# The spectrum step of an FFT and soft-MoE kernel, with constant and data exchanged on TensorE

## The chip, the cores and the metric

The kernel runs on one core of a Trainium2 chip. The metric is device time in microseconds (us) of one execution. The engines are called as in the profile: PE is TensorE's matmuls, PEld its weight loads, DVE is VectorE, ACT is ScalarE, POOL is GpSimd, SP is SyncE, whose queue issues the DMA transfers here. A matmul holds one operand still in the array (the weight, up to 128 rows by 128 columns) and streams the other through it; its result lands in PSUM, out of which DVE and ACT read. A float32 matmul shows as two records in the profile.

## The reference

The input x has 8 batches of 2496 rows of 256 numbers. A filter is applied by a Fourier transform over the rows, and a soft mixture of experts is computed from the result y:

```python
X = np.fft.rfft(x, axis=1)
Y = X * (filt_r + 1j * filt_i)[None]
y = np.fft.irfft(Y, n=2496, axis=1).reshape(8 * 2496, 256)

logits = y @ phi                                  # 32 slots: 8 experts x 4
d = exp(logits - logits.max(0)); d /= d.sum(0) + 1e-09
slot_input = (d.T @ y).reshape(8, 4, 256)
slot_out[e] = relu(slot_input[e] @ w1[e]) @ w2[e]   # for every expert e
c = exp(logits - logits.max(1)); c /= c.sum(1) + 1e-09
out = c @ slot_out
```

All of it is float32.

## The kernel before

**The transform.** 2496 is 39 x 64, so a transform over the rows is one of length 39 and one of length 64. The first stage (`first_stage` for batch 0, `s1_unit` at line 356 for the others) does the 39; its result for a batch is 20 values of t by 64 rows by 256 columns, real and imaginary part. For batches 1 to 7 it goes to DRAM and comes back as tiles `ash` with the 64 rows times two parts on 128 partitions; for batch 0 `turn` makes `ash` by transposes.

**The x step.** `x_unit(b, c)` does the second stage for two values of t, ten units per batch and 80 in all. In the kernel before, `ash` is the weight (128 by 128, one half of the columns d at a time) and the constant matrix (`a1` or `b0`, 128 by 128) streams through. The result in PSUM has d on the partitions, and real and imaginary parts of 64 frequencies for each t along the row. Four matmuls of 128 streamed columns make a unit. DVE then multiplies with the filter: two products of 512 columns (lines 455 and 457) and two of 256 columns that add and subtract (458 and 459; in batches 6 and 7 POOL does these two). The result is `yt`, the filtered spectrum with d on the partitions.

**Transposes and logits.** `t_unit(b, c)` transposes `yt` by four matmuls against the identity (line 467), and ACT copies the result to `y` (line 475), the filtered spectrum with frequencies on the partitions. Every second time it also computes the logits of two units: eight matmuls with 32 columns of `phi` as weight and `yt` streaming (line 485), copied by ACT to `lt` (line 495).

**The chain.** `chain(g)` runs for each of five groups of batches, cut into pieces by `yield`: it transposes the logits (ltr), transforms them back to rows (v1, v, lg), takes the maximum and the exponential (mt, mb, d), transforms the result into the frequency domain again (u, u2, dd), and adds up `slot_input` there, as products of `dd` with `y` (s). It never forms y over the rows. In its code all matmuls and transposes go through two helpers, so they have lines 515 and 512 in the profile.

**The order.** The program is written as a loop over slots n, 80 and two more. A slot issues `x_unit(n)`, the first-stage units that `at_slot` gives it, `t_unit(n-2)` with its logits, and one to three chain pieces (`hop_slot`). A scheduler orders the instructions of each engine by a simulated timeline and by priorities; `high_priority` marks the first stage and the logits; `not_before(a, b)` fixes that a comes after b on its engine, and `behind` makes a queue of such instructions. `held` stores the last instruction of a step for such orders. PSUM has two buffers each for x, for t and l together, and for the chain; the first stage has one of two banks. `ypool` holds 34 units of `y` in rotation.

**Signs.** Frequencies above the half need the filter's imaginary part with the other sign. `make_signs` spreads the signs over all partitions by ten matmuls during batch 0's first stage (line 755), ACT copies them (757), and `sign_tables` multiplies the table `ff_t` with them (line 765), the first two units on DVE, the other eight on POOL. The constants come from `shape_constants`, the filter tables from `filter_layout`.

**Start and end.** `keep_warm(WM)` issues two matmuls on zeros before the first data is there (line 313). After the last slot the rest of the chain goes in the order that `TAIL` writes out; then come the experts' matmuls and the output.

Of the kernel before, what the change touches and what calls it, by code (L numbers as in the profile page):

```python
# [56 lines left out]
LT = 2  # L57
# [31 lines left out]
def shape_constants():  # L89
# [51 lines left out]
    put("sgn", sgn.reshape(NT // 2, P))  # L141
# [39 lines left out]
def filter_layout(filt):  # L181

    idx = np.array([[freq_of(t, c) for c in range(N2)] for t in range(NT)])
    a = filt[np.minimum(idx, SEQ - idx)]
    a = np.ascontiguousarray(a.reshape(NT, N2, 2, P).transpose(3, 0, 2, 1))
    return a.reshape(P, NT // 2, 256)
# [66 lines left out]
def fft_soft_moe(ctx, tc, x0, w0, x, ff, phi, wx, cst, w1q, out):  # L253
# [26 lines left out]
    sgn_t = cst_t[:, OFF["sgn"][0] : OFF["sgn"][0] + P]  # L280
# [41 lines left out]
    held = [None, None, None, None, None]  # L322
# [104 lines left out]
    def x_unit(b, c):  # L427
# [3 lines left out]
        ps = ps_x.tile([P, 4, 2, 64], F32, tag="x", name=f"x_{b}_{c}")  # L431
        for k in range(2):
            for dh in range(2):
                ins = pe.matmul(  # L434
                    ps[:, 2 * k + dh].rearrange("q r c -> q (r c)"),
                    ash[:, k, dh * P : (dh + 1) * P],
                    C("a1" if t0 + k else "b0"),
# [10 lines left out]
        frv, fiv = (  # L448
            ff_t[:, c, k].rearrange("q (p o c) -> q p o c", o=1, c=64).broadcast_to([P, 4, 2, 64]) for k in range(2)
        )  # L450
        t2 = prod.tile([P, 4, 2, 64], F32, tag="t2", name=f"t2_{b}_{c}")
        if c % 2 == 0:
            yts[b, c // 2] = prod.tile([P, 2, 4, 2, 64], F32, tag="yt", name=f"yt_{b}_{c}")
        yt = yts[b, c // 2][:, c % 2]
        dve.tensor_tensor(out=t2, in0=ps[:, :, ::-1, :], in1=fiv, op=ALU.mult)  # L455
        add, part = (pool_e, yt) if b >= PA else (dve, ps)
        dve.tensor_tensor(out=part, in0=ps, in1=frv, op=ALU.mult)  # L457
        add.tensor_tensor(out=yt[:, :, 1, :], in0=part[:, :, 1, :], in1=t2[:, :, 1, :], op=ALU.add)  # L458
        add.tensor_tensor(out=yt[:, :, 0, :], in0=part[:, :, 0, :], in1=t2[:, :, 0, :], op=ALU.subtract)  # L459

    def t_unit(b, c):

        yt = yts[b, c // 2]
        pt = ps_t.tile([P, 2, 2, P], F32, tag="t", name=f"t_{b}_{c}")
        for k in range(2):
            for dh in range(2):
                pe.transpose(pt[:, k, dh, :], yt[:, c % 2, 2 * k + dh].rearrange("q r c -> q (r c)"), ident)  # L467
# [7 lines left out]
        act.copy(y, pt.rearrange("k p h d -> k p (h d)"))  # L475
        ys[b, c] = y
        if c % 2 == 1:
            i = c // 2
            if i == 0:
                lts[b] = work.tile([P, 5, P], F32, tag="lt", name=f"lt_{b}", bufs=2)  # L480
            pl = ps_t.tile([P, P], F32, tag="t", name=f"l_{b}_{i}")
            with tc.high_priority():
                for dh in range(2):
                    for j in range(4):
                        ins = pe.matmul(  # L485
                            pl[32 * j : 32 * j + 32, :],
                            phi_t[:, dh, :],
                            yt[:, j // 2, 2 * (j % 2) + dh].rearrange("q r c -> q (r c)"),
                            start=(dh == 0),
                            stop=(dh == 1),  # L490
                        )
                        if j + dh == 0:
                            not_before(ins, held[1])
            held[2] = ins
            act.copy(lts[b][:, i, :], pl)  # L495
# [21 lines left out]
    def chain(g):  # L517
# [134 lines left out]
        TG = SA if nb == 2 else HT // 2  # L652
# [10 lines left out]
        for t0 in range(0, HT, TG):  # L663
            n = min(TG, HT - t0)
            pd = psum([P, TG, 2, nb, SLOTS], f"dd_{g}_{t0}")
# [3 lines left out]
            ended[0] = act.copy(dd[:, t0 : t0 + n], pd[:, 0:n])  # L669
            if t0 != 0:  # L670
                yield "dd"
# [21 lines left out]
        terms = [(ti, th, b2) for ti in range(HT) for th in range(2) for b2 in range(nb)]  # L693
        step = 4 * nb
        for k, (ti, th, b2) in enumerate(terms):
            j = k % 4
            t = th * HT + ti
            pe_m(
                pss[32 * j : 32 * j + 32, :],
                dd[:, ti, th, b2, :],  # L700
                ys[bs[b2], t // 2][:, t % 2, :],
# [46 lines left out]
    signs = []  # L748

    def make_signs(c0):  # L750
        n = min(4, NT // 2 - c0)
        ps = ps_c.tile([P, 4, 2, 1, N2], F32, tag="c", name=f"sgn_{c0}")
        for c in range(n):
            one = ident[:, c0 + c : c0 + c + 1].broadcast_to([P, P])
# [382 lines left out]
```

## Time and profile before

| | |
|---|---|
| Median of 3 runs | 379.02 us (378.91 to 382.27) |
| The profiled execution's own time | 379.5 us |
| Its span, first to last instruction | 377.7 us |
| Mean granted TensorE clock | 0.958 |
| Busy share of PE, PEld, DVE, ACT, POOL | 93, 69, 68, 46, 39% |
| HBM traffic | 63.11 MB read, 40.12 MB written |

By time, the span has four parts: batch 0's first stage and its start up to 19 us, the 80 slots from there to about 282 us, the rest of the chain up to 304 us, and the experts and the output up to 377.7 us.

How the profile is read: a row of a group names the line, the engine, the operation, the tiles (out<-in), for a matmul the rows by columns of its weight and then the streamed shape, the count, busy time and the mean ns of one. Records of matmuls overlap, since they are pipelined; so the mean of one record is longer than the time between two. The chain of waits is the work that ended last, followed back from the end; a piece of it has a start, a duration, and what it is. "Granted clock" is the share of full speed that TensorE was given.

### The profile page before, as it was taken

How to read it: one execution, taken by the hardware profiler on the slowest of the kernel's cores; microseconds unless marked ns; L12 is line 12 of the kernel's file. 1: busy time of each engine (PE TensorE's matmuls, PEld its weight loads, DVE VectorE, ACT ScalarE, POOL GpSimd, SP SyncE). 2: the span in 40 equal slices, each digit the busy share in tenths (PEclk: the TensorE clock that was granted, in tenths of full speed). 3: DMA queues.
4: the chain of work that ended last, by engine and by line, in shares of the span. 5: the costliest groups of instructions: out<-in, count | busy, mean ns of one | idle time of the engine just before them, and what ended most of it. 6: DMA issues, size and time to landing. Idle time of an engine off the chain costs nothing.

```text
span 377.7 us, 10582 instructions
## 1 busy us (share of the span) xinstructions
PE 350.9 (93%) x4274; PEld 260.7 (69%) x4274; DVE 256.6 (68%) x519; ACT 175.4 (46%) x357; POOL 148.9 (39%) x180
## 2 busy tenths in 40 slices
PE   8999899699999989999999999899998999989960
PEld 6977577467677657777776787777876635878850
DVE  1576788495987987589697837766674562787540
ACT  3556545345456443545644454433363430766430
POOL 0098745453461634454253654323521302650000
PEclk9999999999999999999999999899999999999555
DMA  8999799799889685968955848333698994599996
GB/s 303 400 393 278 245 329 361 257 349 339 259 277 325 187 290 177 320 208 271 336 160 151 253 140 297 129 105 92 203 389 247 339 316 104 222 416 415 418 416 288
DMA packets 50151, 103.92 MB, mean 275 GB/s; under 512 B 5218, under 2 KB 23394, under 8 KB 47926
## 3 DMA queue, kind: packets, MB, share of 16 engines
q1 hardware_dynamic: 49412, 102.83, 78.9%
q8 instruction: 34, 0.56, 0.6%
q10 hardware_dynamic: 690, 0.42, 0.4%
q14 instruction: 15, 0.12, 0.1%
HBM read 63.11 MB, written 40.12 MB: 273 GB/s over the span
## 4 chain that ended last, share of the span: by engine, by line
PE 82%; DMA 7%; DVE 4%; ACT 2%; issue 1%; POOL 0%; DVEq 0%; ACTq 0%; SPq 0%
PE x L434 20%; PE t L467 10%; PE s L356 10%; PE l L485 6%; DMA out<-ob 5%; PE s L515 5%; PE u L515 4%; PE v L515 4%; PE s L407 3%; PE lg L515 3%; PE dd L515 2%; PE out L1087 2%; PE h L1031 2%; PE o L1049 2%; DVE ob L1092 2%; PE v L512 2%
## 5 line engine op out<-in xcount | busy, mean ns | idle before, releaser
L434 PE MATMUL x<-cst_t,ash 128*128 128x128 f32 x640 | 87.8, 280 | 6.2 <-DMA ash<-a_dram 4.1
L434 PEld LDWEIGHTS x<-cst_t,ash 128*128 128x128 f32 x640 | 78.1, 191 | 15.0 <-issue 8.3
L455 DVE TENSOR_TENSOR t<-x,ff_t 128x512 f32<-128x512 f32 x80 | 54.8, 687 | 48.6 <-PE x L434 34.2
L335 POOL TENSOR_TENSOR eo<-xt 128x512 f32<-128x512 f32 (+1 forms) x40 | 48.1, 1203 | 93.0 <-issue 89.6
L365 ACT COPY at<-s 128x1024 f32<-128x1024 f32 (+1 forms) x42 | 39.6, 942 | 48.3 <-PE s L356 34.6
L467 PE MATMUL t<-cst_t,yt 128*128 128x128 f32 x320 | 50.8, 281 | 1.5 <-POOL yt L459 1.4
L467 PEld LDWEIGHTS t<-cst_t,yt 128*128 128x128 f32 x320 | 36.2, 141 | 22.6 <-issue 9.8
L338 POOL TENSOR_TENSOR eo<-xt 128x512 f32<-128x512 f32 (+1 forms) x40 | 48.4, 1211 | 0.0
L475 ACT COPY y<-t 128x512 f32<-128x512 f32 x58 | 33.4, 589 | 24.1 <-PE t L467 22.2
L356 PE MATMUL s<-eo,w1q_t 64*64 64x512 f32 (+1 forms) x336 | 42.8, 579 | 0.0
L457 DVE TENSOR_TENSOR x<-x,ff_t 128x512 f32<-128x512 f32 x60 | 41.5, 695 | 1.2
L1087 PE MATMUL out<-so,st 32*128 32x256 f32 x468 | 35.5, 337 | 2.0 <-ACT ob L1092 1.0
L1087 PEld LDWEIGHTS out<-so,st 32*128 32x128 f32 x468 | 31.0, 222 | 5.8 <-ACT ob L1092 2.9
L1092 DVE COPY ob<-out 128x512 f32<-128x512 f32 (+1 forms) x40 | 25.0, 670 | 8.5 <-DMA out<-ob 5.8
L458 POOL TENSOR_TENSOR yt<-yt,t 128x256 f32<-128x256 f32 x20 | 15.0, 752 | 37.0 <-DVE yt L457 25.3
L1092 ACT COPY ob<-out 128x512 f32<-128x512 f32 (+1 forms) x40 | 21.7, 582 | 14.8 <-DMA out<-ob 7.9
L458 DVE TENSOR_TENSOR yt<-x,t 128x256 f32<-128x256 f32 x60 | 25.2, 420 | 1.9 <-PE l L485 0.2
L485 PE MATMUL l<-yt,phi_t 128*32 128x128 f32 x640 | 26.2, 278 | 0.0
L459 DVE TENSOR_TENSOR yt<-x,t 128x256 f32<-128x256 f32 x60 | 24.9, 414 | 0.0
L495 ACT COPY lt<-l 128x128 f32<-128x128 f32 x40 | 10.7, 268 | 30.4 <-PE l L485 30.0
L485 PEld LDWEIGHTS l<-yt,phi_t 128*32 128x32 f32 x640 | 15.4, 109 | 8.6 <-issue 5.3
L515 PE MATMUL s<-y,dd 128*32 128x256 f32 x232 | 19.3, 381 | 0.4 <-ACT dd L669 0.3
(120 smaller groups left out, 492.1 us busy)
## 6 DMA issues: line engine op xcount, KB each, us to landing
xt<-in_x SPq DMA_DIRECT2D x35, 512.0 KB
ash<-a_dram SPq DMA_DIRECT2D x70, 256.0 KB
out<-ob SPq DMA_DIRECT2D x17, 1024.0 KB
a_dram<-at SPq DMA_DIRECT2D x56, 240.0 KB
w<-in_wx SPq DMA_DIRECT2D x33, 256.0 KB
w<-in_wx SPq DMA_DIRECT2D x6, 512.0 KB
x_t<-in_x SPq DMA_DIRECT2D x5, 512.0 KB
ff_t<-in_ff SPq DMA_DIRECT2D x10, 256.0 KB
```

Of the source, the lines that this page charges most:

```text
L335: ins = eng.tensor_tensor(out=eo[:, 0, 0:n], in0=xs[:, :, 0], in1=xs[:, :, 1], op=ALU.add)
L338: ins = eng.tensor_tensor(out=eo[:, 1, 0:n], in0=xs[:, :, 0], in1=xs[:, :, 1], op=ALU.subtract)
L356: ins = pe.matmul(ps, w1q_t[q, c], eo[q, c, 0:n], start=True, stop=True)
L434: ins = pe.matmul(ps[:, 2 * k + dh].rearrange("q r c -> q (r c)"), ash[:, k, dh * P : (dh + 1) * P], C("a1" if t0 + k else "b0"), start=Tr ...
L455: dve.tensor_tensor(out=t2, in0=ps[:, :, ::-1, :], in1=fiv, op=ALU.mult)
L457: dve.tensor_tensor(out=part, in0=ps, in1=frv, op=ALU.mult)
L458: add.tensor_tensor(out=yt[:, :, 1, :], in0=part[:, :, 1, :], in1=t2[:, :, 1, :], op=ALU.add)
L467: pe.transpose(pt[:, k, dh, :], yt[:, c % 2, 2 * k + dh].rearrange("q r c -> q (r c)"), ident)
L485: ins = pe.matmul(pl[32 * j : 32 * j + 32, :], phi_t[:, dh, :], yt[:, j // 2, 2 * (j % 2) + dh].rearrange("q r c -> q (r c)"), start=(dh = ...
L515: line(pe.matmul(*a, **k))
L1087: nc.tensor.matmul(prs[k][:, mm, :], sts[n][q, hs, c0 : c0 + P], so[q, ho], start=(i == 0), stop=(i == 2))
L1092: copy(ob[:, nm * k : nm * (k + 1), :], prs[k])
```

## The change

The x step exchanges the two operands. The constant is the weight now, in two halves of 64 columns (r = 0 is the real part, r = 1 the imaginary part), and `ash` streams through with all 256 columns d. The two values of t of a unit go to two halves of the partitions: t = 2c to partitions 0 to 63, t = 2c + 1 to 64 to 127. It is still four matmuls a unit. The result has frequencies on the partitions, and DVE's and POOL's products and sums write `y` itself.

`t_unit` transposes `y` by four matmuls as before, and ACT copies the result to `yt`, which only the logits read. The logits are a step of their own now, `l_unit`, with the same eight matmuls, after the first-stage units of its slot. The order in a slot is: `t_unit(n-2)`, `x_unit(n)`, first stage, `l_unit(n-2)`, chain pieces. `t_unit(n-2)` is tied behind `x_unit(n-1)`, and `x_unit(n)` behind `t_unit(n-2)`.

Since the rows of `y` now hold the two values of t of a unit, the chain's `dd` is made to match: four matmuls with 64 columns of `b1` as weight in place of one with 128, in pieces of even length, and the sum `s` runs over (c, r, b2). The marks in `TAIL` follow.

The signs are one number per partition and unit now: a constant of 128 by 10, and one `tensor_scalar` on the table for each unit. `make_signs` is gone, and the warm-up matmuls stream 384 columns, not 512.

```diff
-    (2, "s4"), (1, "u2_0"), (1, "u2_5"), (1, "dd"),
+    (2, "s4"), (1, "u2_0"), (1, "u2_6"), (1, "dd"),
...
-    put("sgn", sgn.reshape(NT // 2, P))
+    put("sgn", sgn.reshape(NT // 2, P).T)
...
-        ps = ps_x.tile([P, 4, 2, 64], F32, tag="x", name=f"x_{b}_{c}")
-        for k in range(2):
-            for dh in range(2):
+        ps = ps_x.tile([P, 2, DIM], F32, tag="x", name=f"x_{b}_{c}")
+        for r in range(2):
+            for k in range(2):
                 ins = pe.matmul(
-                    ps[:, 2 * k + dh].rearrange("q r c -> q (r c)"),
-                    ash[:, k, dh * P : (dh + 1) * P],
-                    C("a1" if t0 + k else "b0"),
+                    ps[64 * k : 64 * k + 64, r],
+                    C("a1" if t0 + k else "b0", 64 * r, 64 * r + 64),
+                    ash[:, k],
                     start=True,
                     stop=True,
                 )
...
-                if k + dh == 0:
+                if k + r == 0:
+                    if held[5] is not None:
+                        not_before(ins, held[5])
...
+        dve.tensor_tensor(out=t2, in0=ps[:, ::-1, :], in1=fiv, op=ALU.mult)
+        add, part = (pool_e, y) if b >= PA else (dve, ps)
+        dve.tensor_tensor(out=part, in0=ps, in1=frv, op=ALU.mult)
+        add.tensor_tensor(out=y[:, 1, :], in0=part[:, 1, :], in1=t2[:, 1, :], op=ALU.add)
+        add.tensor_tensor(out=y[:, 0, :], in0=part[:, 0, :], in1=t2[:, 0, :], op=ALU.subtract)
         ys[b, c] = y
...
+    def t_unit(b, c):
+        if c % 2 == 0:
+            yts[b, c // 2] = prod.tile([P, 2, 2, 2, P], F32, tag="yt", name=f"yt_{b}_{c}")
+        pt = ps_t.tile([P, 2, 2, P], F32, tag="t", name=f"t_{b}_{c}")
+        for r in range(2):
+            for dh in range(2):
+                ins = pe.transpose(pt[:, dh, r, :], ys[b, c][:, r, dh * P : (dh + 1) * P], ident)
+                if r + dh == 0:
+                    not_before(ins, held[0])
+        held[5] = ins
+        act.copy(yts[b, c // 2][:, c % 2], pt)
+
+    def l_unit(b, c):
+        yt = yts.pop((b, c // 2))
...
+                    ins = pe.matmul(
+                        pl[32 * j : 32 * j + 32],
+                        phi_t[:, dh, :],
+                        yt[:, j // 2, dh, :, N2 * (j % 2) : N2 * (j % 2) + N2],
...
-        TG = SA if nb == 2 else HT // 2
+        TG = SA if nb == 2 else 6
...
-            pe_m(pd[:, 0:n], C("b1"), u2[:, t0 : t0 + n], start=True, stop=True)
-            if t0 == 0:
-                pe_m(pd[:, 0, 0], C("bh"), u2[:, 0, 0], start=True, stop=True)
+            for r in range(2):
+                for k in range(2):
+                    o = pd[64 * k : 64 * k + 64, 0 : n // 2, :, r]
+                    pe_m(o, C("b1", 64 * r, 64 * r + 64), u2[:, t0 + k : t0 + n : 2], start=True, stop=True)
+                if t0 == 0:
+                    pe_m(pd[0:64, 0, 0, r], C("bh", 64 * r, 64 * r + 64), u2[:, 0, 0], start=True, stop=True)
...
     def sign_tables(c):
-        (dve if c < 2 else pool_e).tensor_tensor(out=fi, in0=fi, in1=sg.broadcast_to([P, 2, 2, N2]), op=ALU.mult)
+        if c < CPB:
+            fi = ff_t[:, c, 1]
+            eng = dve if c < 2 else pool_e
+            eng.tensor_scalar(out=fi, in0=fi, scalar1=C("sgn", c, c + 1), scalar2=None, op0=ALU.mult)
...
-    keep_warm(WM)
+    keep_warm(WM, 384)
...
     for u in range(NU):
         first_stage(u)
-        if u > 2:
-            make_signs(4 * (u - 3))
...
+        if n >= LT:
+            t_unit(*divmod(n - LT, CPB))
+        if n < NS:
             x_unit(*divmod(n, CPB))
...
         if n >= LT:
             b, c = divmod(n - LT, CPB)
-            t_unit(b, c)
+            if c % 2 == 1:
+                l_unit(b, c)
```

More of the change, by code (lines that the diff above doesn't have):

```diff
@@ L279, in fft_soft_moe @@
     ident = C("id")
-    sgn_t = cst_t[:, OFF["sgn"][0] : OFF["sgn"][0] + P]
     def open_pool(name, bufs, side):
@@ L321, in fft_soft_moe @@
     eos = {}
-    held = [None, None, None, None, None]
+    held = [None] * 6
     def not_before(ins, other):
@@ L447, in x_unit @@
         held[0] = ins
[L448 to L467, printed above, removed]
+        frv, fiv = (ff_t[:, c, k].rearrange("q (o d) -> q o d", o=1).broadcast_to([P, 2, DIM]) for k in range(2))
+        t2 = prod.tile([P, 2, DIM], F32, tag="t2", name=f"t2_{b}_{c}")
         k = (b * CPB + c) % YB - CPB
@@ L474, in t_unit @@
             y = ypool.tile([P, 2, DIM], F32, tag="y", name=f"y_{b}_{c}")
-        act.copy(y, pt.rearrange("k p h d -> k p (h d)"))
-        ys[b, c] = y
[L477 to L495, printed above, removed]
+        dve.tensor_tensor(out=t2, in0=ps[:, ::-1, :], in1=fiv, op=ALU.mult)
@@ new lines, in l_unit @@
+    def l_unit(b, c):
+        yt = yts.pop((b, c // 2))
+        i = c // 2
+        if i == 0:
+            lts[b] = work.tile([P, 5, P], F32, tag="lt", name=f"lt_{b}", bufs=2)
+        pl = ps_t.tile([P, 2, N2], F32, tag="t", name=f"l_{b}_{i}")
+        with tc.high_priority():
+            for dh in range(2):
+                for j in range(4):
+                    ins = pe.matmul(
+                        pl[32 * j : 32 * j + 32],
+                        phi_t[:, dh, :],
+                        yt[:, j // 2, dh, :, N2 * (j % 2) : N2 * (j % 2) + N2],
+                        start=(dh == 0),
+                        stop=(dh == 1),
+                    )
+                    if j + dh == 0:
+                        not_before(ins, held[1])
+        held[2] = ins
+        act.copy(lts[b][:, i, :], pl.rearrange("q r c -> q (r c)"))
@@ L692, in chain @@
         pss = psum([P, DIM], f"s_{g}")
-        terms = [(ti, th, b2) for ti in range(HT) for th in range(2) for b2 in range(nb)]
+        terms = [(c, r, b2) for c in range(HT) for r in range(2) for b2 in range(nb)]
         step = 4 * nb
-        for k, (ti, th, b2) in enumerate(terms):
+        for k, (c, r, b2) in enumerate(terms):
             j = k % 4
-            t = th * HT + ti
             pe_m(
                 pss[32 * j : 32 * j + 32, :],
-                dd[:, ti, th, b2, :],
-                ys[bs[b2], t // 2][:, t % 2, :],
+                dd[:, c, r, b2, :],
+                ys[bs[b2], c][:, r, :],
                 start=(k < 4),
@@ L746, in load_tables @@
         issue(ff_t[:, c], ff[:, c])
[L748 to L754, printed above, removed]
-            behind("pe", pe.matmul(ps[:, c].rearrange("q k o c -> q (k o c)"), one, sgn_t, start=True, stop=True))
-        sg = ypool.tile([P, 4, 2, 1, N2], F32, tag="y", name=f"sg_{c0}")
-        act.copy(sg[:, 0:n], ps[:, 0:n])
-        signs.append(sg)
-    def sign_tables(c):
-        if c >= CPB:
-            return
-        fi = ff_t[:, c, 1].rearrange("q (k h c) -> q k h c", k=2, h=2)
-        sg = signs[c // 4][:, c % 4]
-        (dve if c < 2 else pool_e).tensor_tensor(out=fi, in0=fi, in1=sg.broadcast_to([P, 2, 2, N2]), op=ALU.mult)
+    def sign_tables(c):
+        if c < CPB:
+            fi = ff_t[:, c, 1]
+            eng = dve if c < 2 else pool_e
+            eng.tensor_scalar(out=fi, in0=fi, scalar1=C("sgn", c, c + 1), scalar2=None, op0=ALU.mult)
     NS = BATCH * CPB
```

10 lines of the change are left out of this document (6 added, 4 removed), and 2 rows, old and new, of the table TAIL.

## The prediction

> **What bounds the kernel now.** I read the page's top and its chain of waits first, then busy time by stage, then the groups of instructions by shape, and last the chain row by row, for the price of one block of matmuls.
>
> ```profile
> span 377.7 us, 10582 instructions
> PE 350.9 (93%) x4274; PEld 260.7 (69%) x4274; DVE 256.6 (68%) x519; ACT 175.4 (46%) x357; POOL 148.9 (39%) x180
> PE 82%; DMA 7%; DVE 4%; ACT 2%; issue 1%; POOL 0%; DVEq 0%; ACTq 0%; SPq 0%
> ```
>
> TensorE is the chain. Where it is truly full, the stages tell (us, busy of PE, PEld, DVE, ACT, POOL, then granted clock, DMA share, GB/s):
>
> ```profile
> 19.00:75.00 56.00, 50.91 (x510) 36.67 (x507) 40.94 (x80) 28.39 (x49) 37.76 (x36) 1.00 0.91 310
> 75.00:210.00 135.00, 133.73 (x1626) 95.62 (x1626) 110.00 (x219) 68.06 (x126) 59.30 (x50) 1.00 0.80 260
> 210.00:282.00 72.00, 70.32 (x932) 55.50 (x930) 48.81 (x91) 30.96 (x66) 31.52 (x42) 0.98 0.61 198
> ```
>
> From 19 to 282 us the 80 slots run, each one spectrum unit (x), the transposes of the unit two slots back (t), every second slot a logit block (l), about every second a first-stage block (s at L356), and pieces of the chain. PE lacks 5.1 us of 56 at the start (DMA is at 0.91 there) and 3 us of 207 behind it. So in this stretch a microsecond more of PE is a microsecond more of span. What comes behind 304 us the change does not touch. The blocks, by shape:
>
> ```profile
> L434 PE MATMUL x<-cst_t,ash 128*128 128x128 f32 x640 | 87.8, 280 | 6.2 <-DMA ash<-a_dram 4.1 <-issue 1.1 <-DVE yt L459 1.0
> L434 PEld LDWEIGHTS x<-cst_t,ash 128*128 128x128 f32 x640 | 78.1, 191 | 15.0 <-issue 8.3 <-DVE yt L459 1.8 <-PE z L515 1.1
> L467 PE MATMUL t<-cst_t,yt 128*128 128x128 f32 x320 | 50.8, 281 | 1.5 <-POOL yt L459 1.4
> L515 PEld LDWEIGHTS v<-cst_t,lsb 128*64 128x64 f32 x240 | 7.9, 137 | 2.9 <-issue 1.7 <-DVE t L455 0.8
> ```
>
> Eight records (four matmuls, two records each) make an x unit, four records a t. What matters is the time from one block to the next, and the chain of waits gives it, since PE has no gap in this part (start, duration, block):
>
> ```profile
> 203.33 0.44 PE l L485 x16
> 203.76 1.29 PE s L515 x24
> 205.06 1.09 PE x L434 x8
> 206.15 1.02 PE s L356 x8
> 207.17 0.59 PE t L467 x4
> 207.76 0.89 PE x L434 x8
> 208.65 0.44 PE t L467 x4
> 209.09 0.55 PE ltr L512 x5
> 209.63 0.89 PE x L434 x8
> 210.52 0.57 PE l L485 x16
> 211.10 1.02 PE s L356 x8
> ...
> 152.59 0.97 PE v L515 x28
> 157.01 1.43 PE v L515 x44
> ```
>
> The same block costs two prices. An x behind a t or ltr (same form, 128 rows by 128 columns) takes 0.89; behind the chain's s (128 by 32) it takes 1.09. A t behind x takes 0.44, behind the first stage (64 by 64) 0.59. An l behind x takes 0.57, in the middle of the chain's s (same form) 0.44. So PE pays for every change of array form: 0.20 into x, 0.15 into t, 0.13 into l. For a 128-by-64 form the two v rows give it: 14 pairs in 0.97, 22 pairs in 1.43, so 0.0575 a pair and (0.97 - 14 x 0.0575) = 0.165 for the change. The Trainium skill, TensorEngine Tiling (Array Packing), section Key Properties, says that changing the tiling mode, not merely the tile, drains the engine; it gives no price, and it speaks against this change. The trace agrees, by the 0.13 to 0.20 us above.
>
> **The change part by part.** *Streaming.* x now has the constant as two 64-column weights, side by side in the array, and 256 spectrum columns streaming: still eight records, now in four rounds of two. The trace has no such x. The v rows show that two 64-wide halves do run together (57.5 ns for a pair of 66 columns). The length comes from the chain's s, which streams 256 columns four abreast: 24 records, six rounds, 1.29 us, 0.215 a round. Four rounds are 0.86 against 0.89: 0.03 x 80 = -2.4 us. If two abreast should not overlap, it is 1.72, but the v row excludes that.
>
> *Form changes.* Today x, t, ltr and most chain transposes share one form. I counted every change of form along the PE timeline, between these two rows:
>
> ```profile
> 19.06 1.16 PE L434 MATMUL x<-cst_t,ash 128*128 128x128 f32 x8
> ...
> 282.19 1.03 PE L515 MATMUL u<-cst_t,d 117*32 117x60 f32 x32
> ```
>
> There are 203; 55 of the 80 x units are entered without one, and 38 are left straight into another 128-by-128 block. Afterwards x is 128 by 64, and the new order ties t(n-2) ahead of x(n) and behind x(n-1), so PE alternates t, x, t, x with s and l between. New: 55 entries at 0.165 = 9.1, and 38 exits into a 0.15 entry = 5.7. Back: the 25 entries that are paid already become cheaper, 25 x (0.20 - 0.165) = 0.9; ten places where x touches a v or u piece of 128 by 64 become free, 1.7. That is +12.2 if nothing else moves. The scheduler has 27 pieces of 128 by 64 in this stretch (v, u, and dd, which takes that form too: same columns, same time, one more change at some of its ends); each one that it puts next to x saves one change, so about 25 changes, 4 us, are open: +8 to +12.2. I take +10.
>
> *Start.* The sign matmuls go, and the two warm-up matmuls shrink from 512 to 384 columns:
>
> ```profile
> 1.45 3.74 PE warm_up L313 x4
> 5.19 6.25 PE s L407 x56
> 11.44 0.90 PE sgn L755 x8
> 14.12 0.90 PE sgn L755 x8
> L755 PE MATMUL sgn<-cst_t 128*128 128x128 f32 x20 | 2.7, 276 | 0.0
> ```
>
> All of it is on the chain, with the first stage dense around it: 20 x 0.90/8 = -2.25. The warm-up gives up to 3.74/4 = 0.9 (records at 0.85 apart, a quarter off each), and some back, since the first records of s then run before the clock is full: -0.5, between 0 and -0.9. The signs become a multiply by one number per row on the same engines, DVE twice and POOL eight times:
>
> ```profile
> L765 POOL TENSOR_TENSOR ff_t<-ff_t,sg 128x256 f32<-128x256 f32 x8 | 6.0, 766 | 18.5 <-DMA ff_t<-in_ff 18.5
> L993 POOL TENSOR_TENSOR cr<-c,cst_t 117x96 f32<-117x96 f32 x8 | 2.8, 348 | 0.0
> L988 POOL COPY cr<-c 117x96 f32<-117x96 f32 x8 | 2.1, 263 | 6.9 <-PE ct L1003 6.9
> ```
>
> The new form has one tensor less to read; a copy of one tensor costs POOL 263 where a product of two costs 348, so 766 becomes something between 580 and 766, off the chain as long as POOL finishes its folds before PE asks. I take nothing.
>
> *DVE, POOL, ACT.* The two products and two sums keep their element counts and operands, so nothing. ACT copies the same 512 columns after t. But l now needs that copy:
>
> ```profile
> L475 ACT COPY y<-t 128x512 f32<-128x512 f32 x58 | 33.4, 589 | 24.1 <-PE t L467 22.2
> 47.62 2.23 PE x L434 x16
> 240.38 1.01 PE L467 MATMUL t<-cst_t,yt 128*128 128x128 f32 x4 [1.37 <-POOL yt L459]
> 278.76 0.60 PE L467 MATMUL t<-cst_t,yt 128*128 128x128 f32 x4
> 279.29 0.64 PE L485 MATMUL l<-yt,phi_t 128*32 128x128 f32 x16
> ```
>
> From the start of t to the end of its copy is 0.59 + 0.59 = 1.18; x between them covers 0.165 + 0.86 = 1.03, and a first-stage block, where there is one, 1.02 more. So at worst 0.15 to 0.2 in some 20 slots, and the next t can fill it: 0, at most +4. The last l has no x to cover it: today it starts 0.53 behind its t, then 1.18: +0.65, I take +0.5 (0 to 1).
> What t ahead of x newly holds up: x(n), s(n) and l queue behind t(n-2) and so behind y(n-2). For the first six batches x(n) waits for that same DVE work already, since it needs the PSUM buffer of x(n-2). In the last two POOL makes y, and there t waits already once, 1.37 us.
>
> *Waits that take part of it back.* Up to 75 us x waits 4.1 us for ash loads (the L434 row); the wait before 47.62 is the first of them. What PE loses before such a wait is partly waited anyway: -1.5, between 0 and -4.
>
> Sum: -2.4 + 10 - 2.25 - 0.5 + 0.5 - 1.5 = +3.85; with all open ends on one side -1.5 to +12.5. The profiled execution took 379.5 us (span 377.7 and 1.8 around it), 0.5 above the median of 379.0. So 383.4 in the profile's terms, 382.9 by the median; I say **383.2**.
>
> **Rivals.** *No change, about 380.* The scheduler packs the 128-by-64 pieces next to x (+8), and the early ash waits swallow 3 us: 8 - 2.4 - 2.25 - 0.5 - 3 = 0. For it: the 5 us that PE lacks before 75 us; against: those waits follow s and its stores, which move later with PE.
> *Faster, about 375.* One mechanism: the change into x costs nothing, because its weights are constants and are there before ash is. Then the new entries (9.1) vanish and the old 25 entries, 5.0 us at 0.20, with them; the place is every t-to-x seam. With 10 - 9.1 - 4.1 = -3.2 in place of +10 the sum is -3.2 - 2.4 - 2.25 - 0.5 + 0.5 = -7.85, of which the ash waits, now longer, take back 3 to 4: about 375. The sum changes sign when 80 entries at a price p cost 3.85 less than the 9.1 + 4.1 = 13.2 they stand for: below p = 0.117. Against: l's weights (phi) are constants too, and l pays 0.13. A stronger form of it: the load of weights itself is the price. By the rows, a 128-column load is 191 ns and a 64-column one 137; were each exposed, eight loads a unit would save 0.43, 34 us in all, and the time would be 345. Against it: eight records with eight such loads take 0.89, 0.11 each, less than the load, so loads run under the stream. The Trainium skill, TensorE: Matmul & The Clock Gate, section The mechanism (under packing small matmuls), states that a weight load overlaps a running matmul only if it is for another row group; x uses all rows, so by that rule the loads would be exposed, and the result would be that 345. The trace disagrees, with the same 0.11.
> *Much slower, about 388.* In the last two batches t waits for POOL, PE falls idle, and the clock halves as here behind the wait at 240.38:
>
> ```profile
> 240.50:244.00 3.50, 3.50 (x54) 3.17 (x56) 3.19 (x8) 2.24 (x6) 1.27 (x2) 0.51 0.14 51
> ```
>
> One such window costs 3.5 x (1 - 0.51) = 1.7 us besides its wait of 1.37; one more gives 383 + 3 = 386, two 389.
>
> **Chances.** About 1% (3.8 us) is what a measurement of this kernel can tell from no change. Forecast 0.42 (three quarters of it above 382.8, as its own spread is about 3 us), no change 0.28, faster 0.18 (0.02 of it the 345), much slower 0.12. So slower 0.42 x 0.75 + 0.12 = 0.44, the same 0.28 + 0.10 = 0.38, faster 0.18. The likeliest case alone spans 380 to 387; to leave out no more than two in ten the range goes from 375.5, into the faster case, to 388, short of the second window.
>
> **What would show it.** Right: the chain shows x at 1.02 (0.86 + 0.165) almost everywhere and t at 0.59 almost everywhere; x groups as 128*64 with 256 columns; no sgn; x starts about 2.7 us earlier than 19.06; PE full from 75 to 210. Wrong: x at 0.86 behind t (changes are free into x), x at 1.7 (no pairing), PE waiting for ACT at l or for POOL at t, or a count of changes that stays near 203.

## The result, and the profile after

The changed kernel took 399.7 us (median of 4 runs, 399.25 to 399.96) against 379.6 us for the kernel before, run beside it: a ratio of 1.052, with a 95% interval of 1.048 to 1.056. It is slower, by 20 us where 4 were forecast. Its profiled execution has a span of 398.1 us against 377.7, so 20.4 us are to be found.

The top of the changed kernel's page, and the last line of these three, the chain's shares by engine:

```profile
span 398.1 us, 10672 instructions
PE 377.4 (95%) x4342; PEld 230.4 (58%) x4342; DVE 264.2 (66%) x519; ACT 177.4 (45%) x354; POOL 151.2 (38%) x180
PE 78%; DMA 6%; DVE 6%; ACT 3%; issue 1%; SPq 1%; POOL 0%; DVEq 0%; ACTq 0%
```

The time is on TensorE: its busy time grew by 26.5 us, while the weight loads shrank by 30.3 (each of x's weights has half the columns now). No other engine grew by more than 8 us.

Busy time by stage, changed kernel (us, then busy of PE, PEld, DVE, ACT, POOL, granted clock, DMA share, GB/s):

```profile
19.00:75.00 56.00, 55.56 (x523) 28.24 (x521) 42.52 (x82) 29.21 (x49) 38.15 (x35) 1.00 0.92 311
75.00:210.00 135.00, 133.76 (x1499) 73.25 (x1498) 103.80 (x197) 64.39 (x117) 54.77 (x46) 1.00 0.75 242
210.00:282.00 72.00, 71.46 (x869) 41.84 (x861) 48.27 (x87) 28.49 (x56) 27.72 (x34) 1.00 0.51 159
```

PE is full in each, more so than before, at the full clock: next to nothing new is waited for. In the same 135 us from 75 to 210 it starts 1499 records instead of 1626. The work itself is dearer. How, the chain of waits shows (start, duration, block):

```profile
150.00 0.59 PE t L471 x4
150.59 1.01 PE x L432 x8
151.60 1.02 PE s L354 x8
152.62 0.26 PE ltr L514
152.88 0.57 PE l L487 x16
153.45 0.59 PE t L471 x4
154.04 1.01 PE x L432 x8
155.05 0.26 PE ltr L514
```

In these rows every x costs 1.01 and every t 0.59, which are the prices that the prediction gave them (1.02 and 0.59). Before, a run of t, x, t, ltr, x paid 0.59 (behind s), 0.89, 0.44, 0.55 (for five), 0.89: one entry, and then all in one form. Now each piece has a neighbour of another form on both sides, and a single transpose (ltr) costs 0.26.

For the whole I counted, along the order of the instructions that TensorE is given, the places from the first x to the end of the chain where the array form changes: 204 in the kernel before, 365 in the changed one (by the trace's records 215 and 376). That is 161 more. By the block that is entered (records): x +60, t +35, l +26, ltr +25, dd +8, lg +6, turn +4, others -3.

Where the 20.4 us arose, by the first starts of x units: the first x starts 1.5 earlier (17.58 against 19.06); from there to the 21st unit the changed kernel is 1.0 slower (56.7 us against 55.7) although it makes 36 more changes there; from the 21st to the last unit it is 21.3 slower; behind that it gains 0.5. In the first 20 units PE had idled 5.1 us before and idles 0.4 now, so there most of the added work took the place of waits. The kernel before, then the changed one:

```profile
19.10:74.80 55.70, 50.61 (x509) 36.43 (x505) 40.94 (x80) 28.29 (x49) 37.66 (x36) 1.00 0.92 311
17.60:74.30 56.70, 56.26 (x530) 28.67 (x526) 42.14 (x80) 29.36 (x51) 39.55 (x36) 1.00 0.92 314
```

So the loss lies in the stretch of 59 units that TensorE alone sets. There I put the time from the start of each block to the start of the next (so with the idle time, which is 2.7 us before and 1.8 after) to the block, and counted the changes on entering it:

| from the 21st x to the last | before: changes, us | after: changes, us | difference |
|---|---|---|---|
| x | 21, 57.9 | 65, 62.7 | +44, +4.8 |
| t | 29, 29.6 | 59, 35.1 | +30, +5.5 |
| l | 27, 17.2 | 47, 25.0 | +20, **+7.8** |
| lg, dd | 4, 14.8 | 16, 18.8 | +12, +4.0 |
| ltr | 2, 5.3 | 19, 5.9 | +17, +0.6 |
| s, u, v and the small ones | 74, 74.3 | 70, 72.7 | -4, -1.6 |
| in all | 157, 199.1 | 276, 220.4 | +119, +21.3 |

(The differences, as rounded, add up to 21.1.) Without l that is 13.3 us for 99 changes, and x streams 59 x 0.03 = 1.8 faster, so about (13.3 + 1.8) / 99 = 0.15 a change, as the chain's prices have it. The row of l is another matter: 0.39 for each further entry. Its groups, first of the changed kernel with x and t:

```profile
L432 PE MATMUL x<-ash,cst_t 128*64 128x256 f32 x640 | 91.3, 392 | 0.2 <-DMA ash<-a_dram 0.2
L471 PE MATMUL t<-cst_t,y 128*128 128x128 f32 x232 | 39.5, 286 | 0.4 <-POOL y L461 0.4
L471 PE MATMUL t<-cst_t,yb 128*128 128x128 f32 x80 | 13.5, 285 | 0.8 <-DVE yb L461 0.8
L487 PE MATMUL l<-yt,phi_t 128*32 128x128 f32 x640 | 36.9, 281 | 1.0 <-ACT yt L475 1.0
```

and l of the kernel before:

```profile
L485 PE MATMUL l<-yt,phi_t 128*32 128x128 f32 x640 | 26.2, 278 | 0.0
```

The same 640 records keep PE busy for 36.9 us instead of 26.2. The timeline of the changed kernel shows why (start, duration, block):

```profile
107.76 0.41 PE L487 MATMUL l<-yt,phi_t 128*32 128x128 f32 x4
108.11 0.28 PE L514 MATMUL mt<-cst_t,cmax 117*32 117x117 f32 x1
108.31 0.63 PE L487 MATMUL l<-yt,phi_t 128*32 128x128 f32 x12
108.87 0.55 PE L471 MATMUL t<-cst_t,y 128*128 128x128 f32 x3
```

The block is torn. Whole, its 16 records go four abreast, one for each quarter of the array's columns, and take 0.57. Here those two quarters whose half of the copy was ready start first, two abreast, and the other twelve follow behind another piece: 0.35 and 0.56 from start to next start, so 0.91. With 0.13 for each entry that is two and four rounds of 0.11, where the whole block has one entry and four rounds (0.57 = 0.13 + 4 x 0.11). Of the 40 logit blocks 30 are begun with the half that is ready.

### The profile page after: what moved, and what is told of

Its sections match the earlier page's. It is cut to its first block, busy times and chain, and to the rows that moved or that the text cites. A ratio compares the mean times of both kernels' runs of the same rounds, so it can differ in the third digit from the quotient of the medians.

```text
span 398.1 us, 10672 instructions
## 1 busy us (share of the span) xinstructions
PE 377.4 (95%) x4342; PEld 230.4 (58%) x4342; DVE 264.2 (66%) x519; ACT 177.4 (45%) x354; POOL 151.2 (38%) x180
## 4 chain that ended last, share of the span: by engine, by line
PE 78%; DMA 6%; DVE 6%; ACT 3%; issue 1%; SPq 1%; POOL 0%; DVEq 0%; ACTq 0%
PE x L432 18%; PE t L471 9%; PE s L354 9%; PE l L487 6%; PE s L517 5%; PE out L1083 4%; PE u L517 3%; PE v L517 3%; PE dd L517 3%; PE s L405 3%; DMA a_dram<-at 3%; PE lg L517 3%; DMA out<-ob 2%; DVE ob L1088 2%; PE h L1027 2%; PE o L1045 2%
## 5 line engine op out<-in xcount | busy, mean ns | idle before, releaser
L432 PE MATMUL x<-ash,cst_t 128*64 128x256 f32 x640 | 91.3, 392 | 0.2 <-DMA ash<-a_dram 0.2
L475 ACT COPY yt<-t 128x512 f32<-128x512 f32 x80 | 46.9, 586 | 36.4 <-PE t L471 35.3
L432 PEld LDWEIGHTS x<-ash,cst_t 128*64 128x64 f32 x640 | 40.0, 136 | 26.8 <-issue 12.9
L336 POOL TENSOR_TENSOR eo<-xt 128x512 f32<-128x512 f32 (+1 forms) x40 | 48.7, 1219 | 0.0
L471 PE MATMUL t<-cst_t,y 128*128 128x128 f32 x232 | 39.5, 286 | 0.4 <-POOL y L461 0.4
L487 PE MATMUL l<-yt,phi_t 128*32 128x128 f32 x640 | 36.9, 281 | 1.0 <-ACT yt L475 1.0
L487 PEld LDWEIGHTS l<-yt,phi_t 128*32 128x32 f32 x640 | 18.8, 108 | 25.2 <-issue 15.7
L471 PEld LDWEIGHTS t<-cst_t,y 128*128 128x128 f32 x232 | 25.2, 141 | 13.9 <-issue 10.5
L460 POOL TENSOR_TENSOR y<-y,t 128x256 f32<-128x256 f32 x18 | 13.1, 728 | 40.5 <-DVE y L459 38.3
L517 PE MATMUL s<-y,dd 128*32 128x256 f32 x232 | 18.8, 381 | 0.3 <-ACT dd L675 0.2
L460 DVE TENSOR_TENSOR y<-x,t 128x256 f32<-128x256 f32 x40 | 16.8, 421 | 1.6 <-PE s L517 0.6
L354 PEld LDWEIGHTS s<-eo,w1q_t 64*64 64x64 f32 x336 | 8.8, 131 | 14.9 <-issue 13.6
```

The costliest lines, as they stand in the source:

```text
L336: ins = eng.tensor_tensor(out=eo[:, 1, 0:n], in0=xs[:, :, 0], in1=xs[:, :, 1], op=ALU.subtract)
L354: ins = pe.matmul(ps, w1q_t[q, c], eo[q, c, 0:n], start=True, stop=True)
L432: ins = pe.matmul(ps[64 * k : 64 * k + 64, r], C("a1" if t0 + k else "b0", 64 * r, 64 * r + 64), ash[:, k], start=True, stop=True,)
L471: ins = pe.transpose(pt[:, dh, r, :], ys[b, c][:, r, dh * P : (dh + 1) * P], ident)
L475: act.copy(yts[b, c // 2][:, c % 2], pt)
L487: ins = pe.matmul(pl[32 * j : 32 * j + 32], phi_t[:, dh, :], yt[:, j // 2, dh, :, N2 * (j % 2) : N2 * (j % 2) + N2], start=(dh == 0), stop ...
```

## The experiments

In each diff only the core is shown. Times are medians with the ratio to the kernel before on the same chip and its 95% interval; "changes" is the count along TensorE's order, 204 in the kernel before and 365 in the changed one; idle is PE's idle time from the first x to the end of the chain in the profiled execution, 9.8 us before and 4.6 after. It matters for every price worked out from two times: where more work swallows a wait, the price is net of that wait.

| run | changes | idle, us | time, us | ratio |
|---|---|---|---|---|
| e1_before_x64 | 343 | 5.3 | 397.8 | 1.049 (1.043 to 1.056) |
| e2_after_x128 | 260 | 7.2 | 384.1 | 1.013 (1.007 to 1.019) |
| e3_after_untied | 319 | 9.7 | 399.25 | 1.054 (1.048 to 1.060) |
| e4_before_order | 203 | 9.4 | 378.0 | 0.997 (0.994 to 1.000) |
| e5_after_l | 326 | 8.2 | 394.3 | 1.041 (1.035 to 1.047) |
| e6_after_pairs | 236 | 23.7 | 398.6 | 1.053 (1.046 to 1.061) |
| e7_before_pairs | 184 | 24.6 | 398.0 | 1.051 (1.046 to 1.056) |
| e8_before_nosign | 204 | 8.6 | 378.5 | 0.997 (0.993 to 1.001) |
| e9_before_dummy64 | 340 | 6.0 | 402.5 | 1.059 (1.054 to 1.064) |
| e10_before_dummy68 | 212 | 10.4 | 393.1 | 1.035 (1.030 to 1.041) |
| e11_before_odd | 191 | 8.4 | 375.0 | 0.986 (0.982 to 0.990) |
| e12_after_xxtt | 243 | 11.9 | 385.7 | 1.015 (1.010 to 1.020) |

**The form alone, put into the kernel before.** x keeps its operands and its result, but each matmul is split into two with 64 columns of weights.

```diff
-                ins = pe.matmul(
-                    ps[:, 2 * k + dh].rearrange("q r c -> q (r c)"),
-                    ash[:, k, dh * P : (dh + 1) * P],
...
+                for h in range(2):
+                    d0 = dh * P + 64 * h
+                    ins = pe.matmul(
+                        ps[64 * h : 64 * h + 64, 2 * k + dh].rearrange("q r c -> q (r c)"),
+                        ash[:, k, d0 : d0 + 64],
...
```

> The kernel before, with one thing changed: each weight of the x step (128 columns of the spectrum) is split into two of 64 columns, which go to the two halves of the array; order, dependencies, signs, transposes and logits stay as they were. In the instructions that TensorE is given, the changes of array form between the first x and the end of the chain go from 204 to 343. Theory (the time is paid for changes of form): 105 entries into x at 0.145 us in place of 25 at 0.195, 40 more into t and 16 more into the chain's transposes and its other 128-wide blocks at 0.15, less 2 us of streaming: +16 us, 394 to 398 us. Rival (the new order and the logits' wait for ACT's copy cost the time): nothing of that is in this kernel, so 377 to 381 us.

Measured 397.8 us: the form by itself costs 18.5 us, nearly as much as the whole change, with neither the written order, the signs nor the transposed result changed. The chain of this kernel:

```profile
150.91 1.02 PE s L356 x8
151.93 1.02 PE t L469 x8
152.95 0.55 PE ltr L514 x5
153.50 1.89 PE x L436 x30
155.39 0.57 PE l L487 x16
```

Two x units together take 1.89 = 1.02 + 0.86 (some records are missing in the trace): the first pays the entry, the second doesn't, and two 64-column halves abreast stream in 0.86. Two t units take 1.02 = 0.59 + 0.44 in the same way. 139 more changes cost 18.5 us in the medians, and 80 x 0.03 = 2.4 are gained by streaming: (18.5 + 2.4) / 139 = 0.15 a change. That is net: PE idles 4.5 us less than in the kernel before, and with these it is 0.18. l is not torn here (17.9 us in the stretch of the table above, against 17.2 before), but some x units are: the 59 units there lie in 91 pieces. So this loss and that of the changed kernel are near each other without having the same parts.

**The form alone, taken out of the changed kernel.** x with full 128-column weights, all else as changed.

```diff
-        for r in range(2):
-            for k in range(2):
-                ins = pe.matmul(
-                    ps[64 * k : 64 * k + 64, r],
-                    C("a1" if t0 + k else "b0", 64 * r, 64 * r + 64),
...
+        for k in range(2):
+            ins = pe.matmul(ps[:, k], C("a1" if t0 + k else "b0"), ash[:, k], start=True, stop=True)
```

> The changed kernel, with the x step back in the 128-by-128 form: two matmuls a unit with the whole constant as weight and 256 spectrum columns streaming, so the same streaming time, the same order, the same wait of the logits for ACT. The rows then hold real and imaginary parts of one t, not two t, so the numbers that follow are not the reference's; the amount of work is the same. Changes of form go from 365 to 260 (x 83 to 6, t 75 to 64, chain transposes 29 to 18). Theory (changes of form): 105 fewer at about 0.146 us, -15 us, 383 to 387 us. Rival (order and ACT): no gain, 396 to 401 us.

Measured 384.1 us: 15.6 of the 20 us are gone, 0.15 for each of the 105 changes taken away. The chain:

```profile
154.24 0.59 PE t L464 x4
154.83 0.86 PE x L431 x4
155.69 1.02 PE s L354 x8
156.71 0.59 PE t L464 x4
157.30 0.86 PE x L431 x4
```

Behind t, in t's form, x costs 0.86: 256 columns of stream and no entry. What is left over the kernel before is not x and not t: in the stretch of the table x takes 55.3 us here (57.9 before), t 29.7 (29.6), but l 24.8 (17.2), with its blocks torn as in the changed kernel. l's 7.6 are more than the stretch's whole excess of 6.9.

**The ties of order.** The changed kernel without the two lines that hold t ahead of x and x ahead of the next t.

```diff
-                    if held[5] is not None:
-                        not_before(ins, held[5])
...
-                if r + dh == 0:
-                    not_before(ins, held[0])
```

> The changed kernel without the two orders that tie the transposes of a slot between x(n-1) and x(n); the scheduler places them where it likes. Changes of form go from 365 to 319 (x 83 to 70, t 75 to 62, chain transposes 29 to 15). Theory (changes of form): 46 fewer at about 0.15 us, -7 us, 391 to 394 us. Rival (the tie makes TensorE wait for y, by as much as the whole loss): below 385 us. Rival (the tie costs nothing): 398 to 401 us.

Measured 399.25 us: no gain, although 46 changes went. The expectation failed. The group of x shows part of what took them (busy, mean ns, then the idle time before it and who ended it):

```profile
L432 PE MATMUL x<-ash,cst_t 128*64 128x256 f32 x640 | 90.2, 390 | 6.8 <-DMA ash<-a_dram 5.1 <-issue 1.5
```

Against 0.2 us in the changed kernel x now waits 6.8 us, 5.1 of them for its spectrum, and PE's idle time as a whole is 5.1 us longer (9.7 against 4.6). That is most of the some 7 us that 46 changes should bring. Where it went shows by stage: the first 20 units take 58.8 us against 56.7, with 17 changes less and PE idle for 5.2 us of them; from the 21st to the last unit, where PE sets the pace, it is 214.9 against 220.4, so 5.4 us less for 28 changes less, although l stays torn (22.7 us); behind that it is 1.8 longer. So the changes had their price, and what was saved on them came back in large part as waits.

**The order alone, in the kernel before.** t ahead of x in each slot with both ties, and l as a step of its own, x and its form untouched.

```diff
+                    if held[5] is not None:
+                        not_before(ins, held[5])
...
+        if n >= LT:
+            t_unit(*divmod(n - LT, CPB))
+        if n < NS:
             x_unit(*divmod(n, CPB))
...
-            t_unit(b, c)
+            if c % 2 == 1:
+                l_unit(b, c)
```

> The kernel before with the new order alone: in each slot the transposes of two slots back first, tied between x(n-1) and x(n), the logits as a step of their own behind the first stage; x stays 128 by 128 and the logits still read what DVE wrote. Changes of form 203 against 204. Theory (changes of form): 378 to 382 us, no change. Rival (the order and its ties cost the time): 390 us or more.

Measured 378.0 us: where x has t's form, the new order costs nothing. The alternation of t and x is dear only together with the form.

**Whole logit blocks.** The changed kernel with l's matmuls beginning with the half that is copied last, so that the block can't be begun early.

```diff
-                for j in range(4):
+                for j in (2, 3, 0, 1):
```

> The changed kernel with the eight matmuls of a logit block in another order: the two blocks of the later unit first, so that a block cannot begin before both units are transposed and copied. In the changed kernel the scheduler begins 30 of the 40 blocks with the half that is ready, and puts transposes or chain pieces in before the rest. Changes of form go from 365 to 326 (logits 63 to 36, t 75 to 62). Theory (changes of form alone, 0.15 us each): -6 us, 392 to 395 us. Theory with a second cost (a torn block also fills the array badly, an extra round or two of 0.107 us each): 388 to 392 us. Rival (TensorE then waits for ACT's copy instead): 398 us or more.

Measured 394.3 us, in the interval of the count of changes. The group of l:

```profile
L487 PE MATMUL l<-yt,phi_t 128*32 128x128 f32 x640 | 25.9, 279 | 1.5 <-ACT yt L475 1.5
```

Its busy time falls from 36.9 to 25.9, what the kernel before has; in the stretch l goes from 25.0 to 18.5. In the median whole blocks bring 5.3 us. PE idles 3.6 us longer here (8.2 against 4.6: x waits 2.4 for ash, and l 1.5 for ACT's copy), so the work itself is about 9 us shorter. The 39 changes are 5.9 of these at 0.15; the other 3 fit the records that go two abreast instead of four. So the second cost shows in the rows; the time misses the interval of the theory with it, 388 to 392, by less than the added waits (394.3 - 3.6 = 390.7).

**Pairs of units.** If a change costs 0.15, two units of a form in a row should save half of them. First two t, then two x, in the changed kernel (with whole logit blocks) and in the kernel before (with the new order); then two x, then two t in the changed one.

```diff
-        if n >= LT:
-            t_unit(*divmod(n - LT, CPB))
+        if n % 2 == 0:
+            for m in (n, n + 1):
+                if n >= LT:
+                    t_unit(*divmod(m - LT, CPB))
+            for m in (n, n + 1):
+                if n < NS:
+                    x_unit(*divmod(m, CPB))
         if n < NS:
-            x_unit(*divmod(n, CPB))
```

> The changed kernel with the slots taken two at a time on TensorE: transposes of two units, then the x steps of two units; the logits as in the kernel with the whole blocks, and the transposes of the logits last first, so that they go in one block too. All work and all operands are those of the changed kernel. Changes of form 236, against 365 in the changed kernel and 204 before. Theory (changes of form): 32 more than before at 0.15 is +4.8, less 2.4 of streaming and 2.2 of sign matmuls, 377 to 382 us. Rival (TensorE now waits for y of the unit just before, two in a row): 386 us or more.

> The kernel before with the order of pairs: transposes of two units, then the x steps of two units, x 128 by 128 as before. Changes of form 184, against 204 before. Theory (changes of form): -3 us, 375.5 to 378 us. Rival (waits for y eat it): 379 us or more.

> The kernel of e6_after_pairs with the pairs the other way round: two x units first, then the transposes of the two units before them, which gives y two x steps (2 us) more time. Changes of form 243 against 236 there. Theory (that kernel lost 24 us by waiting for y, and not by a price of its pairs): the wait falls by more than half, 383 to 390 us. Rival (PSUM has two buffers for x, so the second x of a pair waits as long as the transposes did): 395 us or more.

Measured 398.6, 398.0 and 385.7 us. The first two missed. Their t groups, the changed kernel's first:

```profile
L471 PE MATMUL t<-cst_t,y 128*128 128x128 f32 x232 | 35.8, 282 | 8.6 <-DVE y L461 5.1 <-ACT yt L475 1.5 <-POOL y L461 1.2
L471 PE MATMUL t<-cst_t,yb 128*128 128x128 f32 x80 | 12.4, 279 | 6.1 <-DVE yb L461 3.9 <-ACT yt L475 1.5 <-DVE m_run L611 0.4
```

```profile
L469 PE MATMUL t<-cst_t,yt 128*128 128x128 f32 x320 | 51.1, 281 | 16.6 <-DVE yt L461 9.7 <-POOL yt L461 5.3 <-DVE m_run L620 0.8
```

The second t of a pair now comes right behind the x pair that its products are made from, and PE stands still for them, and in part for ACT: some 24 us idle in both kernels. In the changed kernel that is 19 us more, what 129 changes less are worth at 0.15; in the kernel before it is 15 us more, against 20 changes or 3 us. (That kernel is 18 us slower, and what makes the other 6 is not shown.) With x first the products of the second unit have the time of two more x steps. The t groups then wait for nothing, and what is left are waits of x, most of them for its spectrum:

```profile
L432 PE MATMUL x<-ash,cst_t 128*64 128x256 f32 x640 | 85.8, 388 | 7.5 <-DMA ash<-a_dram 6.4 <-DVE yb L461 1.1
```

That kernel takes 14.0 us less than the changed one. To get a price it is set against e5, which has whole logit blocks too: it makes 83 changes less and takes 8.7 us less, 3.7 us of added idle time included, so (8.7 + 3.7) / 83 = 0.15 a change again, with the new form of x kept.

**The signs.** The kernel before without its sign matmuls and without the sign multiplications.

```diff
-        if u > 2:
-            make_signs(4 * (u - 3))
...
     def sign_tables(c):
-        if c >= CPB:
-            return
+        return
```

> The kernel before without the sign matmuls and without the multiplication of the tables by them, so that the signs are left out of the result; nothing else changes. Theory (they are on the chain): -2.2 us, 376.5 to 377.5 us. Rival (the first 20 units are paced by their data, and wait for it the longer): 378.5 to 380 us.

Measured 378.5 us: no difference that can be told. Its windows up to the first x and over the first ten units:

```profile
0.00:18.40 18.40, 16.30 (x108) 13.51 (x108) 5.97 (x16) 6.45 (x16) 0.20 (x4) 1.00 0.93 350
18.40:47.80 29.40, 27.01 (x272) 19.48 (x268) 20.31 (x40) 16.52 (x29) 18.97 (x16) 1.00 0.92 313
```

and the kernel before over its first ten units:

```profile
19.10:47.60 28.50, 26.93 (x271) 19.38 (x268) 20.23 (x40) 16.48 (x29) 23.72 (x24) 1.00 0.91 306
```

The first x starts 0.7 us earlier, and the eleventh starts 0.2 later than before. With DMA at 0.91 to 0.92 the first units come when their data come; what PE saves ahead of them it waits. The run tests a start that is 0.7 us earlier and not 2.2: TensorE came to full speed at 7.39 us here and at 5.03 in the kernel before (more on this at the end). And by the interval of the medians alone anything from 2.8 us gained to 0.4 lost is open.

**A price by itself.** The kernel before with one tiny matmul (one streamed column) ahead of each x unit: with 64 columns of weights, which makes the form 128 by 64, or with 68, which makes it x's own.

```diff
+        ins = pe.matmul(ps[0:64, 0, 0, 0:1], C("id", 0, 64), C("id", 0, 1), start=True, stop=True)
```

> The kernel before with one matmul more ahead of each x unit: 64 columns of the identity as weight, one column streaming, into a place that the x unit overwrites. Its form is 128 by 64. It is the partner of e10_before_dummy68; the two differ in the width of that weight alone. Changes of form 340. Theory (a change of form costs 0.15 us wherever it comes from): 128 more than in the partner, 18 to 20 us slower than it, about 407 us. Rival (only the x step itself, its operands or its products, is slow in the changed kernel): both within 2 us of each other.

> As e9_before_dummy64, but with 68 columns of the identity, which makes the form 128 by 128, that of x and t around it. Changes of form 212, against 204 before. Both theories: the price of two short records and of the load of 68 columns for each, 0.06 us a record, 80 x 0.12 = 9 us at most, 383 to 389 us.

Measured 402.5 and 393.1 us. The timelines, with 64 columns:

```profile
150.62 0.28 PE L432 MATMUL x<-cst_t 128*64 128x1 f32 x2
150.83 1.16 PE L438 MATMUL x<-cst_t,ash 128*128 128x128 f32 x8
```

and with 68:

```profile
153.38 0.23 PE L432 MATMUL x<-cst_t 128*68 128x1 f32 x2
153.47 1.02 PE L438 MATMUL x<-cst_t,ash 128*128 128x128 f32 x7
```

From the start of the tiny matmul to the start of x it is 0.21 in another form and 0.09 in x's own. Both times lie outside what was expected. The sign of the difference is as expected, the size isn't: 9.3 us between the two for 128 changes. The kernel with 68 columns has 4.4 us more idle time and ran four times at half the clock in its profiled execution, two of these rows being:

```profile
49.60:53.00 3.40, 3.40 (x18) 3.37 (x17) 1.39 (x2) 0.00 (x0) 0.00 (x0) 0.50 0.91 274
192.90:196.30 3.40, 3.40 (x59) 2.88 (x51) 1.08 (x5) 0.89 (x3) 0.00 (x0) 0.50 0.63 232
```

Four such windows cost 4 x 3.4 x 0.5 = 6.8 us. The two profiled executions took 402.4 and 397.6, so 4.8 apart, and with both taken off it is (4.8 + 4.4 + 6.8) / 128 = 0.125 a change. That is one profile's reading, and the pair alone would not settle a price; but the two programs differ in nothing but the width of one weight.

**A schedule that uses the price.** The kernel before with the new order, and its first-stage blocks moved from even to the free odd slots, where no logit block stands, so that runs of t and x stay whole.

```diff
-        at_slot.setdefault(max(0, slot_of(b, u)), []).append((b, u))
+        n = max(0, slot_of(b, u))
+        if n >= 12 and n % 2 == 0 and n - 1 not in at_slot:
+            n -= 1
+        at_slot.setdefault(n, []).append((b, u))
```

> The kernel before with the new order alone (as e4_before_order), and the first-stage units moved one slot forward from even to odd slots where that slot has none, so that they stand beside a logit block. x is 128 by 128. Changes of form 191 against 204 before and 203 in e4_before_order. Theory (changes of form): -2 us against before, 376 to 378 us. Rival (the first-stage units come before their data): 380 us or more.

Measured 375.0 us, against 380.2 for the kernel before, run beside it: faster than both kernels. The chain:

```profile
157.51 0.44 PE t L469 x4
157.95 0.89 PE x L434 x8
158.84 0.44 PE t L469 x4
159.28 0.89 PE x L434 x8
160.17 1.02 PE s L356 x8
```

Four units in a row at their low prices. 13 changes fewer are 2 us at 0.15 of the 5.2 us. In the profiled executions PE also idles 1.4 us less, and the half-clock window at 240.5, which cost the kernel before 1.7 us, is missing. Whether these two make the rest in the medians is not shown.

## Why the prediction was right in kind and wrong in size

*Streaming, -2.4: right.* Two halves abreast run in 0.86 (1.01 to 1.02 less an entry; 1.89 for two units in e1). The rival by which each weight load is exposed, 345 us, is out: x makes eight loads in 0.86. There the rule that the prediction took from the Trainium skill (TensorE: Matmul & The Clock Gate, section The mechanism) differs from the measurement, and the measurement decides; the same section also lets a load run ahead if it goes to a background weight buffer, which the prediction left out and these rows do not contradict.

*Form changes, +10: the step that failed.* The prices held: x at 1.01, t at 0.59, l at 0.57 when it is whole, and 0.15 a change in four comparisons (the stretch without l, e1, e2, and e12 against e5). Three of these are net of waits that came or went, 0.16 to 0.18 without them; e9 against e10 gives 0.125. All of the change gives (20.4 + 1.5 for the earlier start + 2.4 streaming) / 161 = 0.15 too, but there 5.2 us of swallowed waits stand against the half-filled rounds of l. The count didn't. The step was "New: 55 entries at 0.165 = 9.1, and 38 exits into a 0.15 entry", 93 less ten free neighbours and half of the 25 that packing was to save, some 70; it was 161. It counted what x itself touches, and there the 93 were right and the savings were not: x and t have 95 more. It left out that x had been the ground on which other pieces of the same form stood free: the single transposes ltr and the pieces lg and turn now need an entry of their own, 35 together, and dd, which took the narrow form itself and was counted at nothing, 8. In time about half of the miss is l. The prediction asked whether l would wait for the copy by ACT, and the answer, next to nothing, was right (1.0 us). It didn't see that the copy now comes in two, one for each slot, and that the scheduler starts l with the first: 26 more entries, and half-filled rounds. That is 7.8 us in the stretch, and e5 takes 6.5 of it back.

Of these sizes, the first 20 units hide theirs: 36 changes, some 5 us, cost 1.0 there. The -1.5 for waits for ash that take something back was the right mechanism, and too small: x waits 0.2 us for ash where it waited 4.1.

*Signs, -2.25, and warm-up, -0.5: wrong as terms of the sum.* x starts 1.5 earlier instead of 2.7. The first stage starts 0.9 earlier (4.15 against 5.03) and the sign matmuls' 2.25 are gone, but eleven of its records stand 0.21 apart and not 0.11, which is 1.1 us, since full speed came later in this execution, and turn waits 0.65 for ACT instead of 0.20. And an earlier start is worth little by e8, where 0.7 us of it were gone by the eleventh unit, since the first units are paced by data. The prediction had this reason at hand for the changes but not for the signs. What the shorter warm-up brings can't be told: when the clock comes to full speed varies more between runs than the warm-up was shortened (below).

*Waits of t and l at 0: nearly right.* t waits 0.4 us for POOL and 0.8 for DVE, l 1.0 for ACT in all. The +0.5 of the last l is not to be seen apart: from the last x on the changed kernel is 0.5 shorter. The half-clock rival did not happen; the changed kernel's three stages stand at 1.00. That t ahead of x holds nothing up is what e4 shows, 0.997.

*Rivals.* "No change" had packing save the count; the scheduler packed next to nothing under the ties that alternate t and x, and without the ties (e3) 46 changes went but next to no time, since waits came instead. "Faster", by a free change into x, is out by the 1.01. Slower was the right side, at 0.44 in all; but "much slower", at 388, was too low and for another reason: it put the danger in a wait of t with a half clock behind it, and not in the count of changes.

*The sum, redone.* Earlier start -1.5; first 20 units +1.0; then 99 changes at 0.153 = +15.1, l +7.8, streaming -1.8; the end -0.5. That is 20.1 of the 20.4. The price in this sum comes from the same table, so it shows where the time lies; that a change has this price rests on the experiments.

## What to carry to other kernels

Before a block gets another array form, list the whole order of TensorE's blocks with their forms, and count the changes with the new form written in: all those pieces count that had stood free between blocks of the old form, not the ends of the changed block alone. Here a change cost about 0.15 us, and a 64-column form that streamed 3% faster lost 5% in all. Order the matmuls of a block with tiles side by side so that its first one needs the operand that comes last, or the scheduler tears it and its rounds run half empty.

## What the runs showed of the hardware that was not expected

*Half the clock for 3.4 us behind a wait.* The two rows of e10 above are such windows; they follow waits of PE of 1.7 us (1.72 for ash up to 49.34, 1.69 for DVE up to 191.91), as the one of the kernel before at 240.5 follows one of 1.37. The changed kernel, with no wait of PE above 0.9 us in its three stages, has none there. So a wait of PE can cost 1.7 us more than its length. It need not: in the kernel before, waits of 1.60 and 2.47 us for ash (up to 47.6 and 74.7) pass at the full clock, as does one of 2.27 in e3 (up to 48.7). What decides is not shown.

*The start of full speed.* The first-stage records stand 213 ns apart at first and then 112. The same 0.8 us, in the kernel before, the changed one, and e9, in this order:

```profile
6.00:6.80 0.80, 0.80 (x9) 0.80 (x9) 0.00 (x0) 0.68 (x2) 0.00 (x0) 1.00 1.06 411
```

```profile
6.00:6.80 0.80, 0.80 (x7) 0.80 (x7) 0.00 (x0) 0.69 (x2) 0.00 (x0) 1.00 1.08 412
```

```profile
6.00:6.80 0.80, 0.80 (x6) 0.80 (x6) 0.00 (x0) 0.00 (x0) 0.00 (x0) 1.00 1.03 397
```

The step to 112 came at 5.03, 6.61 and 7.51 us; e9 has the warm-up of the kernel before. Over all profiled runs it lies between 4.75 and 7.51 with either warm-up. The granted clock in these rows is 1.00 throughout, so it doesn't show this step.
